# An attention, MoE and FFN kernel: one product moved up in each unit of the FFN, its weight loads issued from POOL, token loads freed of two stores, one addition moved up

## The chip, the cores and the metric

One Trainium2 chip, one core. The metric is device time in microseconds (us) of one execution. TensorE (PE) multiplies, VectorE (DVE), ScalarE (ACT) and GpSimd (POOL) work on tiles element by element, and SyncE (SP), ACT and POOL issue DMA transfers.

## The reference

The output of an attention (8 batches of 576 positions) is laid out as 4608 tokens of 512 numbers, goes through a mixture of experts with one expert a token, and then through a feed-forward network with an ELU between its two products. The change touches the feed-forward network alone:

```python
def _moe2_ref(x, w_in, w_out):      # x 4608 x 512, w_in 512 x 2048, w_out 2048 x 512
    h = x @ w_in
    alpha = 1.0
    g = np.where(h > 0.0, h, alpha * (np.exp(np.minimum(h, 0.0)) - 1.0))
    return (g @ w_out).astype(np.float32)
```

## The kernel before, in words

The class `Ffn` is the last 767 us of the program, from about 673 us on. Each of its two products is cut into 36 units: nine token tiles t of 512 tokens, and four weight units u of 512 columns; unit n is t = n // 4, u = n % 4. A unit is worked out in the manner of Strassen, with seven products P1 to P7 of sums of blocks instead of eight of the blocks. Each product is twelve matmuls of 128x128 by 256 columns (an operand is split in a high part `hi` and a rest `lo`, and three of the four combinations are multiplied: L1251 to L1253 in the first half, `prod_in`; L1265 to L1267 in the second, `prod_out`).

**First half.** P6, P7 and P4 of unit n are summed in one bank of the PSUM tile `bd[n % 3]`, P5 and P3 in its other bank, P1 and P2 in `a[n % 2]`. ACT copies P1 out (`p1s`, into the tile `pu`). DVE adds it to P6 (`u2`, L1302, into the other part of `pu`), makes `h` from P6+P7 and P1 (`u3`, L1306) and adds P5 to it (`c22`, L1310). P4 and P3 come after these two, into the same banks; then `bd_add` (L1314) adds `pu` to both banks. The ELU of the three results c, d and y is Relu, Exp and Tanh on ACT (L1277, L1278, L1282; tiles `ex` and `ey`) and two DVE operations (`stt1` L1286, `stt2` L1291), after which SP stores the tile to `g_d` in DRAM. `tc` orders what shares a tile: an operation that writes `bd` waits for those that came before it in the program and read the same tile.

**Tokens.** For each tile t, ACT loads x from `y_d` (`load_x` L1183, `load_b12` L1186), POOL makes sums of its blocks (`half`, L842 to L845), ACT rounds them to `hi` (L1213), and POOL subtracts to get `lo` (L1216): a unit with u = 0 can't start before.

**Second half.** The same 36 units, with `g_d` loaded by ACT (`load_g` L1192, `load_a21` L1196), sums and `lo` on DVE (`left_sums` L832 to L835, L1216). Every fourth unit `evacuate` adds the banks into `o` (L1450), and POOL scatters the rows to the output (L1455). Around the turn from the first half to the second the operands of the second unit (`prep_second`) are made by DVE and POOL (L1493 to L1496).

**Order.** Everything is recorded as events `ev(slot, function)` of one heap; a slot is about the time of one product, and unit n begins at slot 7n. Each engine runs its instructions in the order of their slots. The weights are 28 loads of 512 KB for the first half (`wu<-wic_d`, L1169) and 28 for the second (`wu<-woc_d`, L1173), seven for each of the four tiles `wu`, all issued by SP between its stores. Issues of SP and ACT take eight completion semaphores in turn, those of POOL have eight of their own; an issue waits until the transfer that had its semaphore before has landed.

Of the kernel before, what the change touches and what calls it, by code (L numbers as in the profile page):

```python
# [10 lines left out]
F32 = mybir.dt.float32  # L11
# [32 lines left out]
NJ = N // 512  # L44
NU = 4
# [130 lines left out]
class Early:  # L176
# [3 lines left out]
    def __init__(self, tc, g, rt, psum):  # L180
        self.tc, self.g, self.rt, self.psum = tc, g, rt, psum
# [666 lines left out]
def phases(ctx, tc, g, q, k, v, phi, w1, w2, w_in64, w_out64, out, order=None, tail=None, prologue=None, stop=False):  # L848
# [10 lines left out]
    pend, later, stores = [], [], []  # L859
    small = Small(m)  # L860
# [76 lines left out]
    with tc.manual_schedule():  # L937
        run(attn_items(order, prologue))
    run(tail or TAIL)
    left_a.close()  # L940
    with tc.manual_schedule():
# [123 lines left out]
    with tc.manual_schedule():  # L1065
        plan.load()
        plan.load()
        for n in range(SEAM, NF1 * NSTEP):
            s, fc = n // NF1, n % NF1
            convert_first(n)  # L1070
            slot(s, fc)
            convert(n)
        plan.at(NF1 * NSTEP)
        second()
        small.p1(0)
        second()
# [12 lines left out]
        small.turn_h(1, f.bd[2][:, 0])
        f.prep_rest()  # L1090
        f.prod_in(0, 1)
        small.p2(1, f.a[1])
        right.close()
        f.run(small)
# [38 lines left out]
class Ffn:  # L1133


    def __init__(self, tc, g, ctx, out):
        self.tc, self.g, self.ctx, self.out = tc, g, ctx, out
        self.wu, self.hi, self.lo = {}, {}, {}
        self.elu_items, self.pu, self.h = {}, {}, {}
        self.ld = tc.nc.sync  # L1140
        self.scatters = []
        for u in range(2):
            self.wu[u] = self.keep([P, 7, 2, 2, CW], F32R, f"wu{u}")
        self.sets(0)
# [21 lines left out]
    def load_wi(self, u, at=None):  # L1166
        for c in at or ORDER_IN:
            pos = LAY_IN[c]
            self.tc.nc.sync.dma_start(self.wu[u][:, pos].bitcast(F32), self.g.wic_d[u, :, pos])  # L1169

    def load_wo(self, u, c):
        pos = LAY_OUT[c]
        self.tc.nc.sync.dma_start(self.wu[u][:, pos].bitcast(F32), self.g.woc_d[u, :, pos])  # L1173

    def x_at(self, t, a, b):
        return self.g.y_d[256 * a : 256 * a + 256, 512 * t + 256 * b : 512 * t + 256 * b + 256].rearrange(
# [1 line left out]
        )  # L1178

    def load_x(self, t):  # L1180
        lo = self.lo[t % 2].bitcast(F32)
        at = ((5, 0, 0), (4, 1, 1), (6, 1, 0))
        return [self.ld.dma_start(lo[:, i], self.x_at(t, a, b)) for i, a, b in at]  # L1183

    def load_b12(self, t, dst, k=slice(0, 2)):
        return self.ld.dma_start(dst, self.x_at(t, 0, 1)[:, k])  # L1186

    def load_g(self, k, idx=(0, 1, 2)):
        t, u = divmod(k, NU)
# [125 lines left out]

    def unit(self, n, ev):
        b = 7 * n
        pe = [(1, 0), (6, 1), (5, 4), (2, 5), (7, 6)]
        pe += [(4, 8), (3, 9)] if n == NU * NJ - 1 else [(4, 9), (3, 10)]
        for c, at in pe:  # L1320
            if n or c > 1:
                ev(b + at, self.prod_in, n, c)
        ev(b + 1.1, self.p1s, n)
        ev(b + 2.9, self.u2, n)
        ev(b + 7.1, self.u3, n)
        ev(b + 7.6, self.c22, n)
        ev(b + 7.3, self.act, n, "c", self.a[n % 2])
        ev(b + 8.6, self.act2, n, "c")
        ev(b + 9.05, lambda: self.act(n, "d", self.h[n]))
        ev(b + 9.9, self.act2, n, "d")  # L1330
        ev(b + 9.6 + 0.8, self.stt1, n, "c")
        ev(b + 10.5, self.stt2, n, "c")
        ev(b + 11.1, self.bd_add, n)
        ev(b + 11.9, self.stt1, n, "d")
        ev(b + 12.5, self.stt2, n, "d")
        ev(b + 12.0, self.act, n, "y", self.bd[n % 3])
        ev(b + 13.55, self.act2, n, "y")
        ev(b + 15.1, self.stt1, n, "y")
        ev(b + 16.0, self.stt2, n, "y")

    def half(self, job, k):

# [9 lines left out]
    def prep_halves(self, t, ev):  # L1352

        b0 = NU * 7 * (t - 1)
        job = Ctx()
        job.b = t % 2
        if t < NJ:
            job.kind, job.sums = "x", right_sums
            ev(b0 + 4.6, self.load_x, t)
        else:  # L1360
            job.kind, job.sums = "g", left_sums
            ev(b0 + 4.6, self.load_g, 0)
        if t == 1:
            b0 += 6.5
        self.halves(job, ev, t, [b0 + 4.65, b0 + 4.7], [b0 + 7, b0 + 13.4], [b0 + 11.4, b0 + 18.35], b0 + 10.45)

    def halves(self, job, ev, t, at_load, at_sum, at_hi, at_raw):
        b, nc = job.b, self.tc.nc
# [73 lines left out]
    def evacuate(self, t, b, ev):  # L1442
        nc = self.tc.nc
        sm, o = self.sm, self.o
        v = [[o[h][:, :, CW * d : CW * d + CW] for d in range(2)] for h in range(2)]
        bank = {c: self.out_bank(c).rearrange("p (s f) -> p s f", s=2) for c in range(1, 8)}
        p1, u = [x.rearrange("p (s f) -> p s f", s=2) for x in sm]

        def add(out, x, y):
            nc.vector.tensor_tensor(out=out, in0=x, in1=y, op=ALU.add)  # L1450

        def scatter(h):
            for s in range(2):
                a = 4 * t + 2 * h + s
                sc = nc.gpsimd.indirect_dma_start(  # L1455
                    out=self.out, out_offset=bass.IndirectOffsetOnAxis(ap=self.g.order[:, a : a + 1], axis=0),
                    in_=o[h][:, s], in_offset=None,
                )
                for old in self.scatters:
                    self.tc.declare_no_dep(sc.ins, old.ins, reason="disjoint rows")  # L1460
                self.scatters.append(sc)
                nc.gpsimd.memset(self.gap, 0.0)

        last = t == NJ - 1
        ev(b + 1.2, lambda: nc.scalar.copy(p1, bank[1]))
        ev(b + 2.05, lambda: add(v[0][0], bank[2], p1))
        ev(b + (4.2 if last else 5.5), lambda: add(u, bank[6], p1))
        ev(b + (5.2 if last else 5.6), lambda: add(p1, bank[7], u))
        ev(b + (5.3 if last else 6.0), lambda: add(v[1][0], bank[4], p1))
        ev(b + 6.5, lambda: add(v[1][1], bank[5], p1))  # L1470
        ev(b + 6.6, lambda: scatter(1))
        ev(b + 6.9, lambda: add(u, bank[5], u))
        late = 0 if last else 4.6
        ev(b + 7.2 + late, lambda: add(v[0][1], bank[3], u))
        ev(b + 7.3 + late, lambda: scatter(0))

# [43 lines left out]
    def run(self, small):  # L1520
        for u in (2, 3):
            self.wu[u] = self.keep([P, 7, 2, 2, CW], F32R, f"wu{u}", "right")
        self.sets(1)
        self.tps = ExitStack()
        self.tp = self.tps.enter_context(self.tc.tile_pool(name="tp", bufs=1, reuse_waits="tile"))
        events, count = [], [0]

        def ev(at, fn, *args):
            count[0] += 1
            heapq.heappush(events, (at, count[0], fn, args))  # L1530

        ev(0.6, lambda: small.finish(self.temp("ey")))
        ev(3.5, lambda: small.turn_y(self.bd[2][:, 1]))
        for u in (2, 3):
            for i, c in enumerate(ORDER_IN):
                ev(3.9 + 8 * (u - 2) + 1.1 * i, self.load_wi, u, (c,))
        for n in range(NU * NJ):
            self.unit(n, ev)
        for t in range(1, NJ + 1):
            self.prep_halves(t, ev)  # L1540
        end = self.base(0)
        for u in range(NU):
            b = 7 * (NU * (NJ - 1) + u)
            free = b + 10.2 if u == NU - 1 else b + 11.2
            for i, c in enumerate(ORDER_OUT_LOAD):
                ev(max(b + 7.2 + i, free if i > 4 else 0), self.load_wo, u, c)
        self.prep_second(ev)
        self.turn_over = end + 9.1
        ev(self.turn_over, self.pools_out)
        ev(end + 5.2, self.load_g, 2)  # L1550
        ev(self.turn_over + 0.01, lambda: self.load_a21(2, self.scr[0][:, 2]))
        for k in range(NU * NJ):
            self.out_set(k, ev)
        while events:
            at, _, fn, args = heapq.heappop(events)
            fn(*args)
# [397 lines left out]
ORDER_IN = (1, 6, 5, 2, 7, 4, 3)  # L1954
# [143 lines left out]
```

## Time and profile before

| | us |
|---|---|
| runs, median (lowest, highest) of 3 | 1444.93 (1443.1, 1445.59) |
| profiled execution, its own time | 1441.88 |
| its span | 1440.0 |
| PE busy, of the span | 1327.5 (92%) |
| DVE busy | 1090.3 (76%) |
| ACT busy | 742.6 (52%) |
| POOL busy | 520.1 (36%) |
| granted clock, mean | 0.969 |

The profiled execution is the one whose rows are shown below; all times in rows are us from the start of its span. A wait is the idle time of an engine just before an instruction, put down to what ended last before it.

### The profile page before, as it was taken

What the parts mean: (1) busy time and instruction counts of PE and PEld (TensorE: products, weight loads), DVE (VectorE), ACT (ScalarE), POOL (GpSimd) and SP (SyncE); (2) the same over time, 40 slices, a digit from 0 to 9 for tenths busy, and PEclk for the clock granted to TensorE, in tenths of its full rate; (3) what the DMA queues carried; (4) which work ended last, traced back from release to release, by engine and by line L of the source; (5) the groups of instructions that cost most, each with busy time, mean ns of one, the idle gap of its engine ahead of it and who ended that gap; (6) DMA issues with size and microseconds to landing.
All of it is one profiled execution on the core that took longest, in us unless ns stands there. A gap on an engine that the chain in (4) does not pass through costs nothing.

```text
span 1440.0 us, 30529 instructions
## 1 busy us (share of the span) xinstructions
PE 1327.5 (92%) x12282; PEld 1280.6 (89%) x12282; DVE 1090.3 (76%) x1597; ACT 742.6 (52%) x1094; POOL 520.1 (36%) x516
## 2 busy tenths in 40 slices
PE   7888798988998999989899999999998999999997
PEld 6666588988988999889899999999988999999997
DVE  5677656677886887864598888989967777787773
ACT  2655553445544554553578777777743333333331
POOL 3222234557665665741353333444420001111111
PEclk9999799999999999999999999999999999999999
DMA  8996763466777767678933333233793343434431
GB/s 305 310 282 200 184 185 106 133 199 215 247 245 229 239 222 241 228 226 287 331 123 124 140 139 132 98 138 123 280 384 132 121 145 119 147 120 144 137 127 59
DMA packets 172435, 271.72 MB, mean 189 GB/s; under 512 B 15325, under 2 KB 103233, under 8 KB 172290
## 3 DMA queue, kind: packets, MB, share of 16 engines
q1 hardware_dynamic: 137250, 199.57, 41.5%
q10 hardware_dynamic: 28816, 50.86, 11.2%
q0 software_dynamic: 6224, 19.29, 4.1%
q8 instruction: 98, 1.61, 0.5%
q14 instruction: 47, 0.39, 0.1%
HBM read 173.91 MB, written 95.78 MB: 187 GB/s over the span
## 4 chain that ended last, share of the span: by engine, by line
PE 42%; DVE 18%; DMA 6%; issue 6%; ACT 4%; POOL 1%; ACTq 0%; SPq 0%; POOLq 0%; DVEq 0%
PE bd L1265 5%; PE bd L1267 5%; PE bd L1266 5%; PE bd L1251 3%; PE bd L1253 3%; PE bd L1252 3%; DVE ex L1291 2%; PE ph L632 2%; DVE ex L1286 2%; DVE ey L1286 2%; DVE c L823 2%; PE ph L633 2%; PE ph L631 2%; PE a L1267 2%; PE a L1265 2%
## 5 line engine op out<-in xcount | busy, mean ns | idle before, releaser
L1251 PE MATMUL bd<-hi,wu 128*128 128x256 f32 x720 | 205.4, 285 | 13.9 <-DVE pu L1302 8.4
L1267 PE MATMUL bd<-wu,lo 128*128 128x256 f32 x720 | 203.5, 283 | 7.9 <-DVE lo L1216 7.9
L1265 PE MATMUL bd<-wu,hi 128*128 128x256 f32 x720 | 204.1, 283 | 6.0 <-DVE o L1450 5.0
L1266 PE MATMUL bd<-wu,hi 128*128 128x256 f32 x720 | 203.0, 282 | 0.0
L1252 PE MATMUL bd<-lo,wu 128*128 128x256 f32 x720 | 202.6, 281 | 0.0
L1253 PE MATMUL bd<-hi,wu 128*128 128x256 f32 x720 | 202.4, 281 | 0.0
L632 PE MATMUL ph<-xl,w1s 128*128 128x288 f32 x500 | 151.5, 303 | 19.0 <-DVE xl L508 19.0
L631 PE MATMUL ph<-xh,w1s 128*128 128x288 f32 x500 | 155.2, 310 | 14.4 <-DVE hl L637 10.2
L636 ACT ACTIVATE hh<-ph 128x288 fp32r<-128x288 f32 x125 | 51.2, 410 | 208.9 <-PE ph L633 204.9
L646 PE MATMUL acc<-hh,w2s 128*128 128x288 f32 x512 | 153.8, 300 | 1.0 <-DVE hl L637 1.0
L1251 PEld LDWEIGHTS bd<-hi,wu 128*128 128x128 f32 x720 | 137.0, 190 | 18.6 <-DVE pu L1302 10.7
L647 PE MATMUL acc<-hl,w2s 128*128 128x288 f32 x512 | 153.5, 300 | 0.0
L648 PE MATMUL acc<-hh,w2s 128*128 128x288 f32 x512 | 153.2, 299 | 0.0
L1455 POOL DMA_INDIRECT out_dram<-o,order x36 | 37.8, 1051 | 318.4 <-DVE o L1450 314.8
L633 PE MATMUL ph<-xh,w1s 128*128 128x288 f32 x500 | 149.7, 299 | 0.0
L1267 PEld LDWEIGHTS bd<-wu,lo 128*128 128x128 f32 x720 | 138.4, 192 | 8.3 <-DVE lo L1216 8.3
L1265 PEld LDWEIGHTS bd<-wu,hi 128*128 128x128 f32 x720 | 138.3, 192 | 7.8 <-DVE o L1450 6.6
L1213 ACT CAST hi<-lo 128x1536 fp32r<-128x1536 f32 (+2 forms) x46 | 66.6, 1449 | 141.7 <-DMA lo<-g_d 75.7
L1266 PEld LDWEIGHTS bd<-wu,hi 128*128 128x128 f32 x720 | 138.3, 192 | 0.0
L1253 PEld LDWEIGHTS bd<-hi,wu 128*128 128x128 f32 x720 | 137.1, 190 | 0.0
L1252 PEld LDWEIGHTS bd<-lo,wu 128*128 128x128 f32 x720 | 137.0, 190 | 0.0
L632 PEld LDWEIGHTS ph<-xl,w1s 128*128 128x128 f32 x500 | 96.4, 193 | 22.4 <-DVE xl L508 22.1
(349 smaller groups left out, 3992.2 us busy)
## 6 DMA issues: line engine op xcount, KB each, us to landing
wst<-in_moe_w_dram SPq DMA_DIRECT2D x72, 512.0 KB, 5.2
lo<-g_d ACTq DMA_DIRECT2D x36, 768.0 KB, 4.5
g_d<-ex SPq DMA_DIRECT2D x72, 256.0 KB, 2.4
g_d<-ey SPq DMA_DIRECT2D x36, 512.0 KB, 3.5
wu<-wic_d SPq DMA_DIRECT2D x28, 512.0 KB, 9.6
wu<-woc_d SPq DMA_DIRECT2D x28, 512.0 KB, 7.5
qt<-in_q_dram SPq DMA_DIRECT2D x16, 576.0 KB, 9.9
kv<-in_k_dram SPq DMA_DIRECT2D x16, 576.0 KB, 7.3
```

The source lines that it names most:

```text
L631: nc.tensor.matmul(ph, w1h[:, kc, f], xh[:, kc, :], start=(kc == 0), stop=False)
L632: nc.tensor.matmul(ph, w1h[:, kc, f], xl[:, kc, :], start=False, stop=False)
L633: nc.tensor.matmul(ph, w1l[:, kc, f], xh[:, kc, :], start=False, stop=(kc == 3))
L646: nc.tensor.matmul(py[dc], wh, hh, start=(fc == 0), stop=False)
L647: nc.tensor.matmul(py[dc], wh, hl, start=False, stop=False)
L648: nc.tensor.matmul(py[dc], wl, hh, start=False, stop=(fc == 7))
L1251: nc.tensor.matmul(o, w[:, 0, k, f], xh[:, k], start=s, stop=False, skip_group_check=True)
L1252: nc.tensor.matmul(o, w[:, 0, k, f], xl[:, k], start=False, stop=False, skip_group_check=True)
L1253: nc.tensor.matmul(o, w[:, 1, k, f], xh[:, k], start=False, stop=k == 1, skip_group_check=True)
L1265: nc.tensor.matmul(o, gh[:, j, t], w[:, 0, j], start=first, stop=False, skip_group_check=True)
L1266: nc.tensor.matmul(o, gh[:, j, t], w[:, 1, j], start=False, stop=False, skip_group_check=True)
L1267: nc.tensor.matmul(o, gl[:, j, t], w[:, 0, j], start=False, stop=last, skip_group_check=True)
```

## The change

In a unit of the first half P5 is issued before P4 and P3 of the unit before it, where it was behind them; P2 and P7 stay behind all of these. `u2`, `bd_add`, the ELU and the preparation of the tokens get slots that go with it; of two DVE operations, `bd_add` and `stt1` of part d change places. The weight loads of `wu2` and `wu3` of the first half and all 28 of the second half are issued by POOL (`self.wq`), the first 14 at once at slot 0.2, the others at slots of their own. The token loads of t = 1 are declared independent of two stores to `y_d` whose columns they don't read. In `evacuate` the addition into `v[0][1]` and its scatter are 2.7 slots earlier. The turn is 0.3 slots later.

```diff
+        f.ends = [stores[-1]]
...
-            self.tc.nc.sync.dma_start(self.wu[u][:, pos].bitcast(F32), self.g.wic_d[u, :, pos])
+            self.wq.dma_start(self.wu[u][:, pos].bitcast(F32), self.g.wic_d[u, :, pos])
...
+    def apart(self, ld):
+        for store in self.ends:
+            self.tc.declare_no_dep(ld.ins, store.ins, reason="disjoint columns")
...
-        pe = [(1, 0), (6, 1), (5, 4), (2, 5), (7, 6)]
-        pe += [(4, 8), (3, 9)] if n == NU * NJ - 1 else [(4, 9), (3, 10)]
+        last = n == NU * NJ - 1
+        pe = [(1, 0), (6, 1), (5, 2), (2, 5), (7, 6)]
+        pe += [(4, 8), (3, 9)] if last else [(4, 10), (3, 11)]
...
-        ev(b + 2.9, self.u2, n)
+        ev(b + 3.1, self.u2, n)
         ev(b + 7.1, self.u3, n)
         ev(b + 7.6, self.c22, n)
-        ev(b + 7.3, self.act, n, "c", self.a[n % 2])
...
-        ev(b + 11.1, self.bd_add, n)
-        ev(b + 11.9, self.stt1, n, "d")
-        ev(b + 12.5, self.stt2, n, "d")
...
+        ev(b + 8.3, self.act, n, "c", self.a[n % 2])
...
+        ev(b + 11.6, self.stt1, n, "d")
+        y = b - 2 if last else b
+        ev(y + 12.1, self.bd_add, n)
+        ev(b + 13.0, self.stt2, n, "d")
...
-        late = 0 if last else 4.6
+        late = 0 if last else 1.9
...
+        self.wq = self.tc.nc.gpsimd
         for u in (2, 3):
-            for i, c in enumerate(ORDER_IN):
-                ev(3.9 + 8 * (u - 2) + 1.1 * i, self.load_wi, u, (c,))
+            ev(0.2, self.load_wi, u)
...
-                ev(max(b + 7.2 + i, free if i > 4 else 0), self.load_wo, u, c)
+                ev(max((end - 20.8, end - 11.5, end - 1.5, end + 10)[u] + (1.3, 1.4, 1.6, 1.5)[u] * i, free if i > 4 else 0), self.load_wo, u, c)
...
-        self.turn_over = end + 9.1
+        self.turn_over = end + 9.4
```

Three places show it. The first is PE in a unit of the middle (u = 2; `bd_9778` is its tile, `bd_9777` that of the unit before, `wu_9850` its weights and `wu_9717` those of the unit before). The last matmuls of P6 and the first of what follows, before:

```order
L1251 MATMUL bd_9778<-hi_9858,wu_9850 128x256
L1252 MATMUL bd_9778<-lo_9862,wu_9850 128x256
L1253 MATMUL bd_9778<-hi_9858,wu_9850 128x256
L1251 MATMUL bd_9777<-hi_9858,wu_9717 128x256
L1252 MATMUL bd_9777<-lo_9862,wu_9717 128x256
```

and of the change, at the same place:

```order
L1267 MATMUL bd_9778<-hi_9858,wu_9850 128x256
L1268 MATMUL bd_9778<-lo_9862,wu_9850 128x256
L1269 MATMUL bd_9778<-hi_9858,wu_9850 128x256
L1267 MATMUL bd_9778<-hi_9858,wu_9850 128x256
L1268 MATMUL bd_9778<-lo_9862,wu_9850 128x256
```

What follows P6 was P4 of the unit before; now it is P5 of the unit itself, and P4 stands a product later (lines of the change are 16 higher).

The second is DVE in one turn of evacuations (`o` is the tile for the output, `scr` and `lo` the operands of the next unit, `bd_9778` the bank of P3). Before:

```order
L832 TENSOR_TENSOR scr_14360<-scr_14360,lo_9725 128x512
L833 TENSOR_TENSOR scr_14360<-scr_14360,lo_9725 128x512
L834 TENSOR_TENSOR scr_14360<-lo_9725,scr_14360 128x512
L835 TENSOR_TENSOR scr_14360<-lo_9725,scr_14360 128x512
L1216 TENSOR_TENSOR lo_9725<-lo_9725,hi_9721 128x1536
L1216 TENSOR_TENSOR lo_9725<-scr_14360,hi_9721 128x2048
L1450 TENSOR_TENSOR o_14355<-bd_9778,sm_14358 128x2x256
```

and of the change:

```order
L832 TENSOR_TENSOR scr_14353<-scr_14353,lo_9725 128x512
L833 TENSOR_TENSOR scr_14353<-scr_14353,lo_9725 128x512
L834 TENSOR_TENSOR scr_14353<-lo_9725,scr_14353 128x512
L835 TENSOR_TENSOR scr_14353<-lo_9725,scr_14353 128x512
L1468 TENSOR_TENSOR o_14348<-bd_9778,sm_14351 128x2x256
L1232 TENSOR_TENSOR lo_9725<-lo_9725,hi_9721 128x1536
L1232 TENSOR_TENSOR lo_9725<-scr_14353,hi_9721 128x2048
```

The addition that reads the bank of P3 has moved in front of the two subtractions.

The third is the queue of SP at the turn, before (`wu_9717` to `wu_9854` are the weights of units u = 1, 2, 3):

```order
L1173 DMA wu_9850<-woc_d 128x1024
L1173 DMA wu_9854<-woc_d 128x1024 x2
L1294 DMA g_d<-ey 256x1x512
L1173 DMA wu_9854<-woc_d 128x1024 x2
L1294 DMA g_d<-ex 128x512
L1173 DMA wu_9854<-woc_d 128x1024 x2
L1294 DMA g_d<-ex 128x512
L1173 DMA wu_9854<-woc_d 128x1024
L1294 DMA g_d<-ey 256x1x512
```

and the queue of POOL at the same place in the change, where they now are:

```order
L1174 DMA wu_9717<-woc_d 128x1024 x4
L1174 DMA wu_9850<-woc_d 128x1024 x4
L1513 TENSOR_TENSOR sc<-lo_9725,sc 128x512
L1514 TENSOR_TENSOR sc<-lo_9725,pu 128x512
L1174 DMA wu_9850<-woc_d 128x1024 x2
L1232 TENSOR_TENSOR lo_9725<-pu,hi_9721 128x1024
L1174 DMA wu_9850<-woc_d 128x1024
L1232 TENSOR_TENSOR lo_9725<-sc,hi_9721 128x1024
L1174 DMA wu_9854<-woc_d 128x1024 x7
```

On SP only the stores are left; on POOL the loads stand among the sums and the subtractions of `prep_second`.

## Rows read from the trace of the kernel before

**Rows 1.** Busy time of each engine in four stretches (us from the start).
```profile
core 0: us, PE busy (x) PEld busy (x) DVE busy (x) ACT busy (x) POOL busy (x), PEclk, DMA share, GB/s
673.00:760.00 87.00, 79.50 (x632) 76.96 (x631) 64.43 (x71) 56.33 (x80) 34.58 (x24) 0.98 0.66 234
760.00:1000.00 240.00, 234.49 (x1958) 232.09 (x1957) 217.24 (x233) 183.66 (x250) 102.41 (x72) 1.00 0.36 130
1047.00:1090.00 43.00, 33.99 (x257) 33.08 (x257) 25.83 (x28) 18.25 (x20) 8.61 (x4) 0.91 0.88 328
1090.00:1400.00 310.00, 305.05 (x2593) 303.42 (x2592) 240.52 (x245) 110.53 (x71) 36.13 (x62) 1.00 0.39 132
```

**Rows 2.** Waits of PE, 673 to 1050: us in total, times, longest.
```profile
PE bd L1251 <- DVE pu L1302: 8.4, 11, 3.2
PE bd L1251 <- DVE h L1310: 5.5, 9, 0.9
```

**Rows 3.** Waits of PE, 673 to 730.
```profile
PE bd L1251 <- DVE pu L1302: 5.3, 3, 3.2
PE bd L1251 <- DVE h L1310: 0.8, 1, 0.8
```

**Rows 4.** Waits of PE, 1050 to 1440.
```profile
PE bd L1267 <- DVE lo L1216: 7.9, 2, 5.4
PE bd L1265 <- DVE o L1450: 5.0, 8, 0.6
PE bd L1265 <- ACT hi L1213: 1.0, 1, 1.0
```

**Rows 5.** Timeline of PE around 691 (start, duration, what, wait before it).
```profile
690.94 0.28 PE L1252 MATMUL bd<-lo,wu 128*128 128x256 f32 x1
691.06 0.28 PE L1253 MATMUL bd<-hi,wu 128*128 128x256 f32 x1
694.56 0.39 PE L1251 MATMUL bd<-hi,wu 128*128 128x256 f32 x1 [3.22 <-DVE pu L1302]
694.78 0.28 PE L1252 MATMUL bd<-lo,wu 128*128 128x256 f32 x1
```

**Rows 6.** Three stretches with a low granted clock; columns as in rows 1.
```profile
696.10:699.50 3.40, 3.40 (x19) 3.40 (x18) 2.15 (x3) 1.10 (x3) 0.00 (x0) 0.50 0.75 250
...
1068.20:1071.60 3.40, 3.40 (x16) 3.40 (x17) 2.22 (x2) 1.37 (x2) 2.90 (x2) 0.50 1.03 417
...
1088.00:1092.10 4.10, 4.09 (x19) 4.09 (x20) 2.92 (x2) 1.46 (x2) 0.00 (x0) 0.50 0.61 230
```

**Rows 7.** Timeline of POOL, then of DVE, in the first half.
```profile
700.78 0.74 POOL L842 TENSOR_TENSOR sc<-sc,lo 128x256 f32<-128x256 f32 x1 [29.48 <-PE bd L1253]
...
865.48 2.87 POOL L1216 TENSOR_TENSOR lo<-sc,hi 128x1024 fp32r<-128x1024 f32 x1
...
866.11 2.79 DVE L1291 TENSOR_TENSOR ex<-h,ex 128x512 f32<-128x512 f32 x1
```

**Rows 8.** The chain that ended last, 680 to 730: start, us, what.
```profile
681.25 9.14 DMA y_d<-ey
...
706.02 9.74 DMA wu<-wic_d
```

**Rows 9.** The same chain, 1050 to 1092.
```profile
1065.62 8.31 DMA lo<-g_d
...
1074.01 6.09 DMA g_d<-ex
...
1080.26 3.06 DMA scr<-g_d
```

**Rows 10.** Timeline of DVE at an evacuation.
```profile
1155.37 2.29 DVE L1216 TENSOR_TENSOR lo<-scr,hi 128x2048 fp32r<-128x2048 f32 x1 [0.17 <-ACT hi L1213]
1157.58 0.68 DVE L1450 TENSOR_TENSOR o<-bd,sm 128x512 f32<-128x512 f32 x1
```

**Rows 11.** The group of POOL's scatters on the page: busy, mean ns of one, idle before.
```profile
L1455 POOL DMA_INDIRECT out_dram<-o,order x36 | 37.8, 1051 | 318.4 <-DVE o L1450 314.8
```

**Rows 12.** DMA issues of the page: count, KB each, us to landing.
```profile
wu<-wic_d SPq DMA_DIRECT2D x28, 512.0 KB, 9.6
```

More of the change, by code (lines that the diff above doesn't have):

```diff
@@ L1139, in __init__ @@
         self.elu_items, self.pu, self.h = {}, {}, {}
-        self.ld = tc.nc.sync
+        self.ld = self.wq = tc.nc.sync
         self.scatters = []
@@ L1168, in load_wi @@
             pos = LAY_IN[c]
-            self.tc.nc.sync.dma_start(self.wu[u][:, pos].bitcast(F32), self.g.wic_d[u, :, pos])
+            self.wq.dma_start(self.wu[u][:, pos].bitcast(F32), self.g.wic_d[u, :, pos])
     def load_wo(self, u, c):
         pos = LAY_OUT[c]
-        self.tc.nc.sync.dma_start(self.wu[u][:, pos].bitcast(F32), self.g.woc_d[u, :, pos])
+        self.wq.dma_start(self.wu[u][:, pos].bitcast(F32), self.g.woc_d[u, :, pos])
     def x_at(self, t, a, b):
@@ L1180, in load_x, with load_raws @@
     def load_x(self, t):
+        if t == 1:
+            loads = self.load_raws(t)
+            for ld in loads:
+                self.apart(ld)
+            return loads
+        return self.load_raws(t)
+    def apart(self, ld):
+        for store in self.ends:
+            self.tc.declare_no_dep(ld.ins, store.ins, reason="disjoint columns")
+    def load_raws(self, t):
         lo = self.lo[t % 2].bitcast(F32)
@@ L1185, in load_b12 @@
     def load_b12(self, t, dst, k=slice(0, 2)):
-        return self.ld.dma_start(dst, self.x_at(t, 0, 1)[:, k])
+        ld = self.ld.dma_start(dst, self.x_at(t, 0, 1)[:, k])
+        if t == 1:
+            self.apart(ld)
+        return ld
     def load_g(self, k, idx=(0, 1, 2)):
@@ L1322, in unit @@
                 ev(b + at, self.prod_in, n, c)
-        ev(b + 1.1, self.p1s, n)
-        ev(b + 2.9, self.u2, n)
+        ev(b + 1.45, self.p1s, n)
+        ev(b + 3.1, self.u2, n)
         ev(b + 7.1, self.u3, n)
         ev(b + 7.6, self.c22, n)
-        ev(b + 7.3, self.act, n, "c", self.a[n % 2])
[L1328 to L1332, printed above, removed]
-        ev(b + 11.1, self.bd_add, n)
-        ev(b + 11.9, self.stt1, n, "d")
-        ev(b + 12.5, self.stt2, n, "d")
[L1336 to L1339, printed above, removed]
+        ev(b + 8.3, self.act, n, "c", self.a[n % 2])
+        ev(b + 9.6, self.act2, n, "c")
+        ev(b + 10.05, lambda: self.act(n, "d", self.h[n]))
+        ev(b + 10.9, self.act2, n, "d")
+        ev(b + 10.6, self.stt1, n, "c")
+        ev(b + 10.7, self.stt2, n, "c")
+        ev(b + 11.6, self.stt1, n, "d")
+        y = b - 2 if last else b
+        ev(y + 12.1, self.bd_add, n)
+        ev(b + 13.0, self.stt2, n, "d")
+        ev(y + 13.0, self.act, n, "y", self.bd[n % 3])
+        ev(y + 14.55, self.act2, n, "y")
+        ev(y + 15.3, self.stt1, n, "y")
+        ev(y + 16.2, self.stt2, n, "y")
     def half(self, job, k):
@@ L1364, in prep_halves @@
             b0 += 6.5
-        self.halves(job, ev, t, [b0 + 4.65, b0 + 4.7], [b0 + 7, b0 + 13.4], [b0 + 11.4, b0 + 18.35], b0 + 10.45)
+        self.halves(job, ev, t, [b0 + 4.65, b0 + 4.7], [b0 + 7, b0 + 13.4], [b0 + 12.4, b0 + 19.35], b0 + 11.45)
     def halves(self, job, ev, t, at_load, at_sum, at_hi, at_raw):
@@ L1532, in run @@
         ev(0.6, lambda: small.finish(self.temp("ey")))
-        ev(3.5, lambda: small.turn_y(self.bd[2][:, 1]))
+        ev(3.5, lambda: self.ends.append(small.turn_y(self.bd[2][:, 1])))
+        self.wq = self.tc.nc.gpsimd
         for u in (2, 3):
-            for i, c in enumerate(ORDER_IN):
-                ev(3.9 + 8 * (u - 2) + 1.1 * i, self.load_wi, u, (c,))
+            ev(0.2, self.load_wi, u)
         for n in range(NU * NJ):
```

## The prediction

> **What bounds the kernel now.** I read the waits of PE first, then the busy time by stages, then the chain that ended last. From 760 to 1000 us PE is busy for 234.49 of 240, at full clock; from 1090 to 1400 for 305.05 of 310 [rows 1]. So PE bounds the FFN. What a change of order can give is PE's idle time: the waits in [rows 2, 4], the clock that fell after three of them [rows 6], and no more. The reader is to see that each line of waits has one cause, and that the change has a part for nearly each.
>
> A wait costs a little more than its listed time. Matmuls start 0.12 us apart (690.94, 691.06). The wait listed with 3.22 puts 3.50 between two starts (691.06 to 694.56), 3.38 more than usual, and the next start is 0.22 behind instead of 0.12 [rows 5]. So each wait costs its time and about 0.26. A product is 12 x 0.12 = 1.44 us.
>
> **The change part by part.** In four sums, each with its bounds.
>
> (a) *The order in the steady first half.* From 673 to 1050 there are 20 waits of 13.9 us [rows 2]; 4 of them, 6.1 us, lie before 730 [rows 3] and belong to (b). The other 16 cost 7.8 + 16 x 0.26 = 12.0 us. Half are P4 waiting for `c22`, half P5 waiting for `u2`. Both DVE operations are late since DVE stands still now and then beside POOL: `stt2` took 2.79 us at 866.11, while POOL's subtraction ran from 865.48 to 868.35 [rows 7]. With P5 in front, `c22` has one product more before P4 needs its bank, 1.44 us against a longest wait of 0.9 [rows 2]. P5 then stands ahead of `u2` in the program and waits for it no more; the next product behind `u2` into the tile that it reads is P7, two products later than P5 was. `u2` has to wait for the end of P5 instead, one product later than before, and `stt1` and `stt2` of parts c and d are queued behind it on DVE, and `bd_add` with the Relu of y on ACT behind that: the stores come later by about a product, and nobody reads them before the second half. `bd_add` and `stt1` of d change places; both still run once. I take 11 of the 12.0: one is left for new short waits. Bounds: 2 if DVE has no time to give (first rival) and 12.0.
>
> (b) *The start.* The chain shows `y_d<-ey` from 681.25, 9.14 us, and behind it the token loads on ACT's queue, on which `p1s` and so `u2` waited: PE's wait of 3.22 [rows 5, 8]. Declared independent, the loads issue before it, and ACT goes on. The wait costs 3.2 + 0.26, and the clock that fell to half behind it another 3.40 - 19 x 0.12 = 1.1 us [rows 6]; together 4.6. The other three waits before 730 are 2.9 us [rows 3] and 0.8 around them; the chain of one goes back to a weight load that SP issued only at 706.02 and that took 9.74 us [rows 8]. POOL issues these loads at once, so it should land sooner, but then all 28 loads of the first half compete with the token loads and among themselves in a stretch in which the DMA engines are busy for 0.66 of 87 us [rows 1]. I take 5 of 4.6 + 3.7 = 8.3. Bounds: -10 (one more landing of 9.6 us [rows 12] on PE's path) and 8.3.
>
> What POOL pays: the trace has no plain load of this size issued by POOL; the nearest row is its scatter, 1.05 us each [rows 11]. Fourteen take 14.7 us. POOL is idle for 29.48 us up to 700.78, when it starts the first sums of the tokens [rows 7], so they are hidden, if the issues don't have to wait long for landings. With eight outstanding the last six wait for those eight back, about one landing of 9.6 us: 673 + 14.7 + 9.6 = 697. Without that cover the sums and PE's unit 4 would be later by what exceeds it. I take nothing, bounds 0 and 9.6, which is the -10 above.
>
> A rule of the Trainium skill speaks against this part. On "SBUF — State Buffer", "A bandwidth-pool intuition that's wrong", it says that a transfer issued from GpSimd took about 620 ns alone and about 3100 ns beside a VectorE copy, since its descriptors wait for a port that VectorE holds. The row does not show it: the 36 scatters were issued beside a DVE that is busy for 240.52 of 310 us [rows 1] and took 1.05 us in the mean [rows 11]; DVE adds and subtracts there and copies nothing. By the page's 3100 ns 14 issues would take 43 us, an estimate, and the 5 us of (b) would turn into a loss; the mechanism is the fourth rival, priced there from rows.
>
> (c) *The turn.* Three waits, 7.9 and 1.0 us [rows 4], with 3 x 0.26 make 9.7, and the clock behind two of them took 3.40 - 16 x 0.12 = 1.5 and 4.09 - 19 x 0.12 = 1.8 [rows 6]: 13.0 us. The longest, 5.4, has a chain that is plain: SP's store `g_d<-ex` was issued at 1074.01, when `lo<-g_d` (from 1065.62, 8.31 us) had landed; it took 6.09, and only then ACT issued `scr<-g_d`, 3.06 us [rows 9], for the sums and the `lo` on which PE waited. SP's queue had weight loads between the stores and the eight semaphores ran through them, so a store waited for a transfer that had nothing to do with it. With the loads on POOL, SP issues only stores, and the transfers of the stretch, whose DMA share is 0.88 [rows 1], are spread: 1.3 to 1.6 slots a load instead of 1. If the store is out some 5.4 us earlier, the wait is gone with its clock: 5.4 + 0.26 + 1.8 = 7.5. The other wait for `lo`, 2.5 with 0.26 and 1.5 for the clock, hangs on a 768 KB load in the same crowd; half of it, 2.1, may go. The wait for `hi` (1.0) stays. 7.5 + 2.1 = 9.6; POOL has its two `lo` of the turn now queued behind loads of about 1 us, so I take 9. Bounds: 2 and 13.0.
>
> (d) *The evacuation.* Eight waits of 5.0 us in total, none over 0.6 [rows 4], cost 5.0 + 8 x 0.26 = 7.1. P3 of the next turn waits for the addition that reads its bank, and this stood at 1157.58 behind a subtraction of 2.29 us from 1155.37 [rows 10]. Moved in front of both subtractions it ends some 4 us sooner, and the wait of 0.6 is over. What is late next is `lo` of the next unit, by the 0.6 us that an addition takes, with most of a unit to spare. I take 7.0. Bounds 6 and 7.1.
>
> Sum: 11 + 5 + 9 + 7 = 32, less 2 for what POOL's fuller queue may cost somewhere: 30. All of it, 12.0 + 8.3 + 13.0 + 7.1, would be 40.4. From the profiled 1441.88 this makes 1411.9. The median of the runs stands 3.05 above the profiled execution, and the change is independent of that: 1444.93 - 30 = 1415.
>
> **The rivals.**
>
> *DVE becomes the bound.* It is busy for 217.24 of 240 us [rows 1]. If PE's idle 240 - 234.49 = 5.5 us goes, the same work fills 217.24 / 234.5 = 93%, and what it loses beside POOL comes in pieces of 2 us (2.79 for one operation in [rows 7]). For: little reserve. Against: a queue that is 93% full still catches up within a unit, and each deadline has got later. Then (a) is 2 instead of 11: 1415 + 9 = 1424.
>
> *The weights come late at the start.* Three queues then fill the same engines; a load that took 9.6 us on SP [rows 12] may take twice that, and `wu1`, still on SP and wanted earlier by P5, is late. For: 0.66 share over 87 us, with stretches at the limit. Against: the bytes are the same as before, and `wu2` and `wu3` have 20 to 30 us. Then (b) is -10 instead of 5: 1430. The Trainium skill ("DMA: Bandwidth & Descriptors", "Issuing engines are not separate DMA queues") says that transfers run on the same 16 engines whichever engine starts them, which is this rival's reason.
>
> *The change doesn't do what it says.* The waits that go are refilled by others on PE's path (`u2` behind P5, P7 behind `u2`; `lo` behind POOL's issues), so that only (d) is left and lost again at the start: 1445. For it nothing in the rows but the size of the rearrangement.
>
> *Slower: POOL's queue holds up the tokens.* POOL runs in order. The sums and subtractions of t = 1 stand behind 14 issues; POOL has 29.48 us for them [rows 7]. The point from which it decides is an issue of 29.48 / 14 = 2.1 us. If an issue stood still beside DVE as DVE did beside POOL, it would take 2.79: 14 end at 673 + 39 = 712, the sums start 11 us later than at 700.78, and PE's unit 4 with them. At the turn 28 loads would take 78 us instead of 29, with the subtractions of `prep_second` among them; half of the excess, 25, lies on PE's path. With the 14 of (b) and (c) gone too this makes 1415 + 14 + 11 + 25 = 1465. For: POOL's order. Against: 1.05 us a scatter beside a busy DVE [rows 1, 11]. Chance 0.07.
>
> **How the numbers follow.** Forecast 0.62, range of its own 1408 to 1422; DVE bound 0.14; weights late 0.12; nothing changed 0.05; POOL's queue 0.07. The range of 1406 to 1431 holds the first three but their edges; the last two, 0.12, are left out. Faster by over 0.2% (2.9 us, about what a measurement of this kernel can tell from no change) are the first three: 0.88; within it 0.05; slower 0.07.
>
> **What would show it.** In the profile after: from 760 to 1000 PE's waits for L1302 and L1310 (now 16 lines further down) nearly gone; no wait of P3 for `o`; SP's stores at the turn issued right behind their DVE operation, PE's longest wait there under 3 us; POOL's 14 issues within 30 us and no wait of PE for `lo` around unit 4. It is wrong if PE's waits for DVE stay at 12 us in the steady part, if weight loads or POOL's issues head PE's waits at 680 to 720, or if the turn still holds a wait of 5 us.

## The result and the profile after

The changed kernel takes 1428.96 us (median of 4 runs, 1426.97 to 1431.16) against 1444.01 of the kernel before on the same chips: a ratio of 0.9896, 95% interval 0.9879 to 0.9912. It is faster by 15 us, half of what was forecast. The profiled execution took 1428.33 us, its span is 1426.6, and its FFN began at 673.88 us where that of before began at 673.71; so all of the difference of 13.4 us lies in the FFN.

Busy time by stretches, columns as in rows 1; the stretch 1000 to 1100 holds the whole turn and stands in for 1047 to 1090, and 1100 to 1400 for 1090 to 1400.

```profile
673.00:760.00 87.00, 78.22 (x621) 76.18 (x621) 58.69 (x68) 54.18 (x76) 40.46 (x35) 0.94 0.64 233
760.00:1000.00 240.00, 240.00 (x2061) 240.00 (x2060) 212.03 (x247) 192.87 (x264) 108.84 (x72) 1.00 0.38 136
1000.00:1100.00 100.00, 84.92 (x677) 83.91 (x676) 81.69 (x75) 55.30 (x65) 39.76 (x44) 0.93 0.73 262
1100.00:1400.00 300.00, 300.00 (x2571) 300.00 (x2570) 235.06 (x240) 106.79 (x68) 54.16 (x64) 1.00 0.41 137
```

The kernel before did this in 1000 to 1100 and in 1100 to 1400:

```profile
1000.00:1100.00 100.00, 90.08 (x721) 88.59 (x719) 76.37 (x80) 59.87 (x73) 26.53 (x17) 0.95 0.75 274
1100.00:1400.00 300.00, 295.05 (x2514) 293.42 (x2513) 232.97 (x238) 105.89 (x69) 36.13 (x62) 1.00 0.39 132
```

The reader is to count matmuls. PE without a pause does 2061 of them in 240 us, so each is worth 0.1164 us; the prediction and the expectations round this to 0.12. In the steady first half there are 2061 instead of 1958 [rows 1]: 103 x 0.1164 = 12.0 us won. From 1100 to 1400 there are 2571 instead of 2514: 6.6 won. At the start 621 instead of 632: 1.3 lost. At the turn 677 instead of 721: 5.1 lost. The sum is 12.2; the rest lies behind 1400. PE has no idle time at all in the two long stretches, and all its waits in the FFN are six (us in total, times, longest):

```profile
PE bd L1267 <- DVE h L1326: 14.1, 4, 7.5
PE bd L1283 <- DVE lo L1232: 8.4, 1, 8.4
PE bd L1267 <- DMA wu<-wic_d: 1.1, 1, 1.1
```

[Rows 2 and 4] had 20 and 11. The long lines of short waits are gone; a few long ones at the start and at the turn are new. The chain that ended last shows the one at the start (start, us, what):

```profile
668.63 14.95 DMA wu<-wic_d
...
683.60 19.50 DMA lo<-y_d
```

The third token load, issued at 683.60 as soon as SP's load had landed, took 19.50 us. PE's wait came by another transfer of the same crowd. SP issued the first two stores `g_d<-ex` at 692.93, right behind DVE, and at 698.05; until the first had landed, ACT had no free `ex` tile, and behind ACT's Relu stood DVE's `stt1` of part d and, in DVE's order, `c22`. The semaphore on which ACT waited got its sixteen steps from this store between 704.02 and 709.32: the store took 16.39 us. SP's row (both stores in one), ACT's row, PE's row behind it, and the issues of POOL meanwhile:

```profile
692.93 5.43 SPq L1310 DMA_DIRECT2D g_d<-ex  x2
```

```profile
709.40 0.63 ACT L1293 ACTIVATE ex<-h 128x512 f32<-128x512 f32 x1 [8.66 <-DMA g_d<-ex]
...
718.02 0.58 PE L1267 MATMUL bd<-hi,wu 128*128 128x256 f32 x1 [7.50 <-DVE h L1326]
```

```profile
682.23 0.53 POOL L1170 DMA_DIRECT2D wu<-wic_d  x1 [2.49 <-DMA wu<-wic_d]
684.75 0.53 POOL L1170 DMA_DIRECT2D wu<-wic_d  x1 [1.99 <-DMA wu<-wic_d]
687.34 0.53 POOL L1170 DMA_DIRECT2D wu<-wic_d  x1 [2.06 <-DMA wu<-wic_d]
```

POOL's issues follow each other at 2.5 to 3 us, each as a load of 512 KB lands, that is at some 190 GB/s, while all other transfers share the rest. What moved from 676 to 716 by queue (q0 is POOL's, q1 SP's; packets, MB, share of the engines' time), first before, then in the change:

```profile
q1 hardware_dynamic: 4372, 12.64, 88.9%
...
q0 software_dynamic: 2016, 7.34, 46.9%
q1 hardware_dynamic: 2304, 5.27, 36.2%
```

In all it is 13.73 MB before and 13.70 in the change: no more was moved, but other transfers came first. At the turn DVE stands still. POOL, then DVE, then PE:

```profile
1017.25 2.66 POOL L1174 DMA_DIRECT2D wu<-woc_d  x5
1019.92 1.87 POOL L1232 TENSOR_TENSOR lo<-lo,hi 128x768 fp32r<-128x768 f32 x1
1021.75 2.41 POOL L1232 TENSOR_TENSOR lo<-sc,hi 128x1024 fp32r<-128x1024 f32 x1
```

```profile
1019.35 5.36 DVE L1307 TENSOR_TENSOR ex<-h,ex 128x512 f32<-128x512 f32 x1
...
1062.85 6.88 DVE L1302 SCALAR_TENSOR_TENSOR ey<-ey 128x1024 f32<-128x1024 f32 x1
1069.66 1.75 DVE L1232 TENSOR_TENSOR lo<-lo,hi 128x1536 fp32r<-128x1536 f32 x1
```

```profile
1071.46 0.58 PE L1283 MATMUL bd<-wu,lo 128*128 128x256 f32 x1 [8.42 <-DVE lo L1232]
```

An operation of 0.69 us began while POOL was issuing and ended at 1024.71, 0.55 behind POOL's second subtraction (1024.16). In the kernel before the longest was 2.79 [rows 7]. All waits of PE from 1000 to 1100, first before, then in the change:

```profile
PE bd L1267 <- DVE lo L1216: 7.9, 2, 5.4
PE bd L1265 <- ACT hi L1213: 1.0, 1, 1.0
PE bd L1251 <- DVE h L1310: 0.5, 1, 0.5
PE bd L1251 <- DVE pu L1302: 0.4, 1, 0.4
...
PE bd L1283 <- DVE lo L1232: 8.4, 1, 8.4
PE bd L1267 <- DVE h L1326: 6.6, 3, 2.8
```

So `lo` costs about what it did, in one wait instead of two, and the three waits for `c22` (h L1326) are new.

### The profile page after: what moved, and what is told of

Its sections match the earlier page's. It is cut to its first block, busy times and chain, and to the rows that moved or that the text cites. A ratio compares the mean times of both kernels' runs of the same rounds, so it can differ in the third digit from the quotient of the medians.

```text
span 1426.6 us, 30491 instructions
## 1 busy us (share of the span) xinstructions
PE 1319.1 (92%) x12282; PEld 1275.7 (89%) x12282; DVE 1078.5 (76%) x1597; ACT 742.8 (52%) x1094; POOL 566.1 (40%) x558
## 4 chain that ended last, share of the span: by engine, by line
PE 51%; DVE 11%; DMA 7%; issue 5%; POOL 3%; ACT 2%; SPq 0%; POOLq 0%; ACTq 0%; DVEq 0%
PE bd L1283 6%; PE bd L1281 6%; PE bd L1282 6%; PE bd L1268 5%; PE bd L1267 5%; PE bd L1269 5%; PE a L1281 2%; PE a L1282 2%; PE a L1283 2%; DVE c L823 2%; PE a L1269 2%; PE a L1268 2%; PE a L1267 2%; DMA lo<-y_d 1%; PE ph L632 1%
## 5 line engine op out<-in xcount | busy, mean ns | idle before, releaser
L1473 POOL DMA_INDIRECT out_dram<-o,order x36 | 54.4, 1512 | 290.9 <-DVE o L1468 287.2
L1267 PEld LDWEIGHTS bd<-hi,wu 128*128 128x128 f32 x720 | 139.0, 193 | 16.4 <-DVE h L1326 14.9
L1269 PEld LDWEIGHTS bd<-hi,wu 128*128 128x128 f32 x720 | 139.2, 193 | 0.0
```

The source lines that it names most:

```text
L1267: nc.tensor.matmul(o, w[:, 0, k, f], xh[:, k], start=s, stop=False, skip_group_check=True)
L1269: nc.tensor.matmul(o, w[:, 1, k, f], xh[:, k], start=False, stop=k == 1, skip_group_check=True)
```

## The experiments

Three theories stood at first. **A**: POOL's issues cost more than they give, at the start by slowing other transfers, at the turn by holding up DVE. **B**: the new order and slots themselves make the start and the turn late. **C**: without POOL, SP's stores are held up again. **D** to **G** came with later runs and are told in their expectations. Each kernel is compared with the kernel before on its own chip. Besides the ratio the table gives the FFN alone, from its first product to the end of the span in the profiled execution, since the part ahead of it, which no edit touches, differs by some us between executions (the FFN begins at 670 to 681). The FFN column is one execution a kernel, and e3's is the fastest of its five (1414.12).

| kernel | median us | ratio (95%) | FFN, us |
|---|---|---|---|
| before | 1444.01 | | 766.3 |
| changed | 1428.96 | 0.9896 (0.9879 to 0.9912) | 752.7 |
| e1, all loads on SP | 1418.2 | 0.9805 (0.9763 to 0.9846) | 741.8 |
| e2, second half's loads on SP | 1423.45 | 0.9854 (0.981 to 0.9898) | 746.4 |
| e3, first half's loads on SP | 1420.82 | 0.9842 (0.9811 to 0.9874) | 738.2 |
| e4, issues apart from subtractions | 1423.83 | 0.9856 (0.9813 to 0.9899) | 747.3 |
| e5, e3 and e4 and a quieter turn | 1417.47 | 0.9826 (0.9801 to 0.9852) | 737.4 |
| e6, order alone | 1427.77 | 0.9887 (0.9868 to 0.9906) | 748.7 |
| e7, addition alone | 1437.37 | 0.995 (0.9926 to 0.9974) | 760.1 |
| e8, tokens alone | 1438.93 | 0.9974 (0.9954 to 0.9993) | 761.3 |
| e9, thin loads at the turn | 1431.64 | 0.9919 (0.9895 to 0.9943) | 748.8 |
| e10, wu3 later | 1427.61 | 0.9891 (0.9857 to 0.9926) | 746.0 |
| e11, POOL's loads in pieces | 1417.72 | 0.982 (0.9796 to 0.9843) | 738.6 |
| e12, e5 with lo first | 1422.25 | 0.9849 (0.981 to 0.9888) | 741.9 |

**All loads back on SP (e1).**

```diff
-        self.wq = self.tc.nc.gpsimd
...
-            ev(0.2, self.load_wi, u)
+            for i, c in enumerate(ORDER_IN):
+                ev(3.9 + 8 * (u - 2) + 1.1 * i, self.load_wi, u, (c,))
...
-                ev(max((end - 20.8, ...)[u] + (1.3, 1.4, 1.6, 1.5)[u] * i, free if i > 4 else 0), self.load_wo, u, c)
+                ev(max(b + 7.2 + i, free if i > 4 else 0), self.load_wo, u, c)
```

> The changed kernel with all weight loads back on SP at the slots of the kernel before; order of products, independent token loads and the earlier addition are kept. Theory A (POOL's issues cost more than they give: at the start they slow the token loads, at the turn DVE stands still through trains of issues and subtractions): the long DVE operations of 5.36, 3.97 and 6.88 us at the turn are gone, the stretch 1000 to 1090 holds at least 50 matmuls more, and the time is 1419 to 1424. Rival B (the losses come from the new order of the products and the later slots of ACT and DVE): the turn and the start stay as they are, 1427 to 1431.

Measured 1418.2: 27.0 us under the kernel before on the same chip, 10.8 under the changed kernel across chips. Theory A holds and B falls in the main: with the same order the queue of the loads, and the slots that go with it, make the difference. Most of it is at the start, where 681 matmuls stand in 673 to 760 instead of 621 (7.0 us). The turn has 707 in 1000 to 1100, 30 more than the changed kernel (3.5 us; 50 were expected), and 14 fewer than the kernel before. DVE's operations of 5.36, 3.97 and 6.88 us are gone.

**Only the second half's loads on SP (e2), only the first half's (e3).** The same edit, once for `load_wo` and once for `load_wi`.

> The changed kernel with only the 28 loads of the second half back on SP at the slots of before; the 14 of the first half stay on POOL. Theory A: the turn loses what it lost before or less (12.8 us of 90 instead of 19.0), the start stays (one wait of about 7.5 near 718): 1422 to 1425. Rival B: 1427 to 1431. Rival C (the loads on SP hold the stores up, which was the 5.4 us wait of before): that wait is back and the gain is eaten, 1426 to 1432.

> The changed kernel with only the 14 loads of wu2 and wu3 back on SP at the slots of before; the 28 of the second half stay on POOL. Theory A: the third token load of t = 1 lands in under 12 us instead of 19.5, the wait near 718 is gone or under 3 us, the turn stays: 1422 to 1426. Rival B: the wait stays, 1427 to 1431. Rival C (on SP they delay the stores and come late themselves): a wait of some 2 us for u2 near 717 as in the kernel before, 1425 to 1428.

Both are faster than the changed kernel by their FFN, e2 by 6.3 us and e3 by 14.5; by their medians, 1423.45 and 1420.82, only e3 is clear of it (the interval of e2's ratio overlaps that of the changed kernel). In e3 PE's waits at the start are

```profile
PE bd L1268 <- POOL lo L1232: 1.2, 1, 1.2
PE a L1268 <- POOL lo L1232: 0.6, 1, 0.6
PE bd L1267 <- DMA wu<-wic_d: 0.5, 1, 0.5
```

and the two stretches

```profile
673.00:760.00 87.00, 84.63 (x697) 82.69 (x696) 66.74 (x78) 60.12 (x85) 34.48 (x24) 1.00 0.68 247
...
1000.00:1100.00 100.00, 87.56 (x716) 86.74 (x715) 80.57 (x77) 51.44 (x57) 47.02 (x51) 0.95 0.78 277
```

So 76 matmuls (8.8 us) come back at the start, and 39 (4.5 us) at the turn, where nothing was edited; that the turn depends on how POOL and DVE happen to meet there is how I read it, no run shows it alone. e2 brings 723 at the turn (x723, two more than before), but its first stall is still there (5.5 for `c22`, and 2.8 for weights). Rival C fell for e3: no wait of 2 us is back. For e2 it half held: two waits for `lo` of 7.8 us in total stand at its turn, the second of them (2.2) the one that was 5.4 before, but the gain is not eaten.

**Issues apart from the subtractions (e4).**

```diff
+                ev((end - 15.3, end - 8.3, end - 1.5, end + 10)[u] + (0.1, 0.7, 0.7, 1.5)[u] * i, self.load_wo, u, c)
```

> The changed kernel with the 28 loads of the second half still on POOL, but none of them directly in front of a subtraction: u0 behind the subtractions of the first half of the last tile, u1 behind those of its second half, u2 before the sums of the second unit, u3 as it was. Theory A in its narrow form (it is the issue in front of the subtractions that keeps DVE out between them): no DVE operation over 3 us at the turn, the waits for c22 there gone, 1420 to 1425. Rival D (DVE is late there since SP's stores land late in a crowd of transfers, whatever POOL's order): ACT still waits 2 to 3 us for g_d<-ex and PE for c22, 1426 to 1432.

Neither side won. DVE's operations of 5.36 and 3.97 us in front of the turn are gone and those at it are 3.36 and 3.89, and 716 matmuls stand in the stretch, 39 more; e6, with no weight load on POOL, has the same two (3.36 and 3.89), so these come from POOL's subtractions alone. But a wait of 3.1 for `c22` and one of 9.0 for `lo` are left, and the chain behind them has `g_d<-ex` with 9.26 us and `lo<-g_d` with 9.63: D has its part too. The time is 1423.83, its interval overlaps the changed kernel's.

**A quieter turn (e5).** e3 with the loads of e4, `u2` behind the subtractions.

```diff
+                ev((end - 15.3, end - 8.3, end + 8.2, end + 10)[u] + (0.1, 0.7, 0.2, 1.5)[u] * i, self.load_wo, u, c)
```

> The changed kernel with wu2 and wu3 of the first half on SP at the slots of before, and the loads of the second half on POOL but held away from the load of the second unit's operand: u0 and u1 behind the subtractions of the last tile, u2 behind those of the second unit, u3 as it was. Theory E (what is left at the turn is a transfer: the 768 KB load for the second unit can't start before the first half has left its buffer, and takes 9 to 10 us in the crowd of weight loads): in a quiet stretch it lands in about 5 us, the wait of the second unit for lo falls from 6 to 9 us to 2 to 4, 1412 to 1417. Rival F (DVE and POOL, not the load, set the wait): it stays at 6 us or more, and u2, loaded later, adds a wait of its own: 1420 to 1426.

1417.47, but not for the reason that was expected: the wait for `lo` is 7.6 and the stretch was not quiet, since POOL had issued fourteen loads just before; the load of the second unit's operand took 9.24 us. Theory E was not tested by it. By the FFN e5 (737.4) is e3 (738.2).

**The parts alone on the kernel before (e6, e7, e8).** e6 takes the slots of `unit` and `prep_halves`, e7 the one line `late = 0 if last else 1.9`, e8 `apart` and its calls.

> The kernel before with the new order and slots of the products and of DVE and ACT alone; loads on SP, the tokens' loads wait for the two stores, the addition late, the turn where it was. If the gain of the steady first half is the order's: no wait of PE for L1302 or L1310 (whatever their lines) from 760 to 1000, 100 matmuls more in that stretch, 1431 to 1435. If it was the queue or the loads that took these waits away: 1440 to 1446.

> The kernel before with the earlier addition of the evacuation alone. If the eight waits for o were the addition's place: they are gone, 1090 to 1400 has no idle time, 1436 to 1439. If something else takes their place: 1442 to 1447. Each scatter beside a subtraction of DVE should take 1.9 to 2.3 us instead of 1.05, off the path.

> The kernel before with the independent token loads of t = 1 alone. If the store to y_d was what held ACT: PE's wait of 3.2 us at 694 and the low clock behind it are gone, the other waits before 730 stay, 1438 to 1442. If the loads wait for something else (a landing eight issues back): the wait stays at over 2 us, 1443 to 1447.

All three do what they were said to do. e6 has no wait of PE from 760 to 1000 and 102 matmuls more there:

```profile
760.00:1000.00 240.00, 240.00 (x2060) 240.00 (x2059) 211.66 (x247) 193.06 (x263) 108.79 (x72) 1.00 0.38 137
```

and at 1427.77 it alone is as fast as the whole change. It won more than expected since it also took most of the stall at the start: ACT was blocked for 8.72 us (10.82 before), but PE waited only 1.06 for it, since P5 no longer stands behind `u2`. e7 took 5.5 us off the median (6.2 off the FFN), without a wait in 1100 to 1400. Of its scatters, those beside DVE's subtractions take longer, 2.23 and 1.90 us as expected, off the path; the mean of all:

```profile
L1455 POOL DMA_INDIRECT out_dram<-o,order x36 | 54.4, 1511 | 294.3 <-DVE o L1450 290.7 <-issue 3.6
```

e8 took 3.9 off the median (5.0 off the FFN); the clock stays at 1.00 at the start, a wait of 2.3 us for `u2` is left at 709. By the FFN the three sum to 17.6 + 6.2 + 5.0 = 28.8; e1, which has all of them, has 24.5: order and tokens take the same stall away.

**Thin loads at the turn (e9).**

```diff
-        self.wq.dma_start(self.wu[u][:, pos].bitcast(F32), self.g.woc_d[u, :, pos])
+        self.wq.dma_start(self.wu[u][:, pos, 0, 0, :128].bitcast(F32), self.g.woc_d[u, :, pos, 0, 0, :128])
```

> The changed kernel with the same 28 issues of the second half's weights on POOL, at the same places, but each moves 64 KB instead of 512: seven eighths of the second half's weights are left out, and PE multiplies what lay in the tiles before. Theory G (the turn is bound by the bytes that have to move there): stores of g land in 2 to 4 us, PE loses under 5 us from 1000 to 1100 instead of 18.8, 1410 to 1416. Rival A (it is the issues on POOL among its subtractions that hold DVE up, whatever they move): DVE operations of 4 to 7 us stay, the waits for c22 and lo too, PE still loses 12 us or more there, 1422 to 1429.

This one decides between A and G. With an eighth of the bytes the DMA share falls to 0.44, and DVE still stands still:

```profile
1000.00:1100.00 100.00, 84.87 (x699) 83.86 (x698) 85.11 (x78) 57.09 (x71) 39.73 (x45) 0.95 0.44 140
```

```profile
1025.11 5.66 DVE L1307 TENSOR_TENSOR ex<-h,ex 128x512 f32<-128x512 f32 x1
...
1038.11 3.95 DVE L1302 SCALAR_TENSOR_TENSOR ex<-ex 128x512 f32<-128x512 f32 x1
...
1065.49 6.87 DVE L1302 SCALAR_TENSOR_TENSOR ey<-ey 128x1024 f32<-128x1024 f32 x1
```

```profile
PE bd L1283 <- DVE lo L1232: 8.8, 1, 8.8
PE bd L1267 <- DVE h L1326: 6.3, 3, 2.6
```

The waits are those of the changed kernel (8.4; 6.6 in three), and PE is busy as long (84.87 us; 84.92). It does 22 matmuls more, 2.6 us, at a granted clock of 0.95 instead of 0.93. Theory G falls for the changed kernel: what keeps DVE standing is the issues and subtractions on POOL, whatever they move. The time, 1431.64, is above the 1422 to 1429 of theory A; its interval overlaps the changed kernel's. The wait for `lo` is not settled by this run, for e6, with the loads on SP, has one as long at its turn:

```profile
PE bd L1276 <- DVE lo L1225: 9.5, 2, 9.1
```

**wu3 later (e10).**

```diff
-            ev(0.2, self.load_wi, u)
+            ev(0.2 if u == 2 else 13.6, self.load_wi, u)
```

> The changed kernel with the seven loads of wu3 still on POOL, but issued behind the first sums of the tokens (slot 13.6 instead of 0.2). If the crowd of POOL's loads is what makes the token loads and the stores late at the start: the last token load lands in 10 to 14 us instead of 19.5, the wait of 7.5 near 718 shrinks to under 4, 1421 to 1426. If any use of POOL's queue there costs it (its issues behind PE or landings): the wait stays at 6 us or more, or PE waits for wu3 itself by more than 3 us, 1427 to 1433.

With fewer loads in flight at the start, PE's longest wait is 2.1 instead of 7.5 and it does 38 matmuls more in 673 to 760 (659). The first `g_d<-ex` took 8.27 us instead of 16.39, the third token load 15.75 instead of 19.50 (10 to 14 were expected). The FFN is 6.7 shorter; by the median, 1427.61 and a ratio whose interval holds that of the changed kernel, it can't be told from it.

**POOL's loads in pieces (e11), and lo first (e12).**

```diff
+            at = (end - 15.3, end - 8.3, end + 8.2, end + 10)[u]
+            for i, c in enumerate(ORDER_OUT_LOAD):
+                ev(end + 4.1 if u == 1 and i > 2 else at + 0.1 * i, self.load_wo, u, c)
```

> wu2 and wu3 of the first half on SP at the slots of before; the second half's loads on POOL, u0 and three of u1 early, the other four of u1 behind the sums of the second unit, u2 and u3 behind its subtractions. Theory E (the load of the second unit's operand must be alone): it lands in 5 to 7 us, PE's wait for lo falls under 4 us, 1411 to 1416. Theory G (the bytes of the turn take their time in any order): the wait goes to another place, PE loses 12 to 15 us from 1000 to 1100 as in the other versions, 1416 to 1422.

The wait for `lo` fell to 0.8, and two waits of 7.7 us in total for the loads that I had put off took its place: 1417.72, as G had it, with 719 matmuls at the turn. The 0.8 is no success of E: PE had waited 7.5 for weights just before, and behind them `lo` was hardly late. The operand's load landed in 6.52 us, as E wanted, but DVE, beside the four issues and the two subtractions that follow them, took 7.36 us for one operation ahead of its `lo`.

```diff
-        ev(e + 6.4, lo, slice(0, 3), nc.vector)
+        ev(e + 4.7, lo, slice(0, 3), nc.vector)
```

> The kernel of the quiet turn (first half's loads on SP, second half's on POOL away from the subtractions) with one more move: DVE's subtraction for the second unit stands two operations earlier, in front of the two that POOL's subtractions hold up. Theory A (what is left at the turn is DVE held up by POOL): PE's wait for lo falls from 7.6 us to under 3 us, the time to 1408 to 1414. If the second unit waits for its transfer or for ACT's hi instead: the wait stays at 5 us or more, 1415 to 1420; if the ELU parts behind it come too late instead, a new wait for a later product of 2 us or more, 1413 to 1418.

On top of e5. The wait for `lo` fell from 7.6 to 2.7, as A said, and what was put behind it came too late:

```profile
PE bd L1281 <- DVE ey L1307: 4.4, 1, 4.4
PE bd L1281 <- DMA wu<-woc_d: 4.0, 2, 2.2
PE bd L1267 <- DVE h L1326: 2.8, 1, 2.8
PE bd L1283 <- DVE lo L1232: 2.7, 1, 2.7
```

1422.25, above the 1408 to 1414 of A and the 1413 to 1418 of the last rival; worse than e5 or the same (the intervals of the ratios overlap).

## Why the prediction was half right

The forecast was 1415 with a range of 1406 to 1431. The time lies in the range, at its far end. That it is near the 1430 of the rival in which the weights come late at the start is chance: the rival kept the 9 us of the turn and lost 10 at the start; here the start lost 1.3 and the turn 5.1. By its steps:

*(a), 11 us for the order: right.* All steady waits went; 12.0 us in 760 to 1000 alone, and e6 shows that the order did it. Rival one (DVE the bound) did not come: DVE is busy for 212.03 of 240.

*(d), 7 us for the addition: right.* 6.6 by the matmuls from 1100 to 1400, 6.2 by the FFN alone in e7.

*(b), 5 us at the start: wrong, it lost 1.3.* Two steps of it held: the token loads went out some 8 us earlier (682.33 instead of 690.46), and POOL's fourteen issues were done at 696.76, where 697 was worked out. That this came out to the microsecond is luck: an issue took 0.54 us instead of the scatter's 1.05, and the waits before the last seven, 2 to 4 us each, came to 18 instead of the 9.6 of one landing. Nor was the 1.05 a price beside DVE's subtractions, where a scatter takes 2.23 and 1.90 (e7). What failed is the step that costed the loads at nothing as long as POOL was free. Their cover was POOL's idle time; the price was paid by others on the same engines: SP's load 14.95 us, the token load 19.50, and the store for which ACT waited 16.39. The prediction reckoned with a DMA share of 0.66, a mean of 87 us; from 676 to 716 SP's queue alone had filled 88.9% of the engines' time in the kernel before, so what POOL's loads took, over half of the bytes there, others had to give. e3 gives 8.8 us of it back at the start, and there the first two stores take 7.6 and 7.7 us. The rival named the place, but PE's wait went by way of a store, not of late weights (1.1 us). Besides, 4.6 us of (b) were counted next to (a), whose order takes most of the same stall by itself (e6); alone on the kernel before, the tokens did bring 5.0 by the FFN (e8).

At the step that failed stands the page's rule that I had kept for the rival alone. The Trainium skill ("DMA: Bandwidth & Descriptors", "Issuing engines are not separate DMA queues") says that issuing from more engines saves only the time of issuing; this case's trace agrees: issuing was 0.54 us a load, and with no more bytes moved (13.70 MB; 13.73) the transfers of SP and ACT took longer.

*(c), 9 us at the turn: wrong, it lost 5.1.* The store was seen as late because of the queue in front of it, and this step held: SP issued its last `g_d<-ex` of the turn at 1062.95, right behind DVE, instead of 1074.01 [rows 9], and no wait of PE stands any more where the one of 5.4 us was. With the order of the change and the loads on SP it does (3.5 in e1, 2.2 in e2, 0.5 in e6). The row of SP, two stores in one:

```profile
1058.21 5.06 SPq L1310 DMA_DIRECT2D g_d<-ex  x2
```

Two other steps failed. The first took a wait that goes for time won. The wait for `lo` ahead of it grew from 2.5 us to 8.4, and the sum stayed: 7.9 before, 8.4 now, and 6.4 to 9.5 in e1 to e10, whichever queue the loads are in. It ended in e1 to e5 with DVE's `lo`, behind POOL's two subtractions (3.9 us instead of 1.75) and behind transfers of 8 to 10 us; reduced in e11 and e12, it came back as waits for weights and for the ELU. The second put too little on POOL's queue: 0.6 us for its `lo` behind the loads, and 2 us for it being fuller. The prediction had the row that points there, 2.79 us of DVE beside POOL [rows 7], and did not ask what issues in front of two subtractions, or between them, do to it: 5.36 and 6.88, and 3.97 for an operation that began beside the first of the two. Two of the three waits for `c22`, 3.8 of their 6.6 us, stand right behind the 5.36 and the 3.97; they are gone, or 0.3, where these are gone (e1, e2, e4), and e9 shows that it is not the bytes. The third, 2.8, is there in e1, e2, e5 and e6 too (2.2 to 3.2), so it comes with the new order and not with the loads.

A rule on DVE beside POOL too: the Trainium skill ("SBUF — State Buffer", "Who interferes with whom") says that a VectorE instruction with two inputs in SBUF contends with a GpSimd instruction that reads SBUF, and that whoever comes first blocks the other. The rows agree, and go further: the DVE operations of 5.36 and 6.88 us were held through two subtractions and the issue before them.

The sign that the prediction had named for being wrong, a wait of 5 us left at the turn, came. In e1 to e5 and e11 the turn costs 100 - 0.1164 x (707 to 723) = 16 to 18 us, and 16 before. Whether these 16 us can be had at all stays open.

## What to carry to other kernels

A wait that repeats every unit and has one cause is worth its rows: both such terms came true within 1 us. A transfer that is moved to another engine's queue is not free when that engine is idle: ask whose transfers it shares the engines with, whether those are wanted sooner, and what the issuing engine's other instructions do to their neighbours. A wait that goes is won only if no other wait of the same chain grows in its place. And when two parts of a change remove the same stall, their gains don't add: try each alone.

## What the runs showed of the hardware

A plain 512 KB load was issued by POOL in 0.54 us. A DVE operation with both inputs in SBUF that began beside a POOL DMA issue followed by two subtractions did not get in between them: 5.36 us instead of 0.69 and 6.88 instead of 1.22, and the same with an eighth of the bytes (5.66, 6.87). In the other direction, scatters beside DVE's subtractions took 2.23 and 1.90 us in e7, where the mean of all before was 1.05. With POOL's loads eight at a time in flight, its queue moved 7.34 of the 13.70 MB from 676 to 716, and a store of 256 KB on SP's queue took 16.39 us.
